# Moving VectorE's sums and output additions to other steps in a fused recurrence and ELU network, with plain products for the last four pairs

## Chip, cores and metric

One Trainium2 chip, one core. The number that counts is the device time of one execution in microseconds; lower is better. All data are fp32. The engines are named as in the profile: PE (TensorE, with PEld its weight loads), DVE (VectorE), ACT (ScalarE), POOL (GpSimd) and SP (SyncE, which only issues DMAs here).

## What is computed

```python
# q, k, v, f_logit: (4, 8, 768, 48)
f = 1.0 / (1.0 + np.exp(-f_logit))
for t in range(S):
    state = f[:, :, t, :, None] * state + np.einsum('bhd,bhe->bhde', k[:, :, t], v[:, :, t])
    y[:, :, t] = np.einsum('bhd,bhde->bhe', q[:, :, t], state)
x = y.transpose(0, 2, 1, 3).reshape(3072, 384)
h = x @ w_in                                   # 384 -> 2048
g = np.where(h > 0.0, h, np.exp(np.minimum(h, 0.0)) - 1.0)
out = g @ w_out                                # 2048 -> 384
```

A gated recurrence gives x for 3072 tokens; two matrix products with an ELU between them follow. "The second product" below is `g @ w_out`.

## The kernel before, in words

**Units, pairs, steps.** The tokens are cut into 12 units of 256 (`m` = 0 to 11). The 2048 hidden features make 16 tiles of 128, taken two at a time, so a unit has 8 pairs (`j` = 0 to 7). A pair over all units has the number P = 8m + j, 0 to 95. The main loop runs over steps T = 0 to 191; step T = 2P makes the first product of pair P (`up`), step 2P + 1 finishes that pair's hidden sums (`joined`) and makes the second product of pair P − 2 (`down`, `LAG = 2`). The place of a step in its unit is called **s = T mod 16** below.

**The order of the work is written by hand.** Each engine executes its instructions in the order in which the program emits them (`manual_schedule`), and waits on semaphores where data or a buffer is missing. `plan` (filled by `at_step`) says which work of the recurrence is emitted at which step. For units 3 to 11 it is, one unit ahead: decays at s = 9, 11, 13, 15 (DVE: a scan and a reciprocal; POOL: scalings of k and q), the x differences `blend` at s = 13 (POOL), `transposed` at s = 2 (PE and ACT), `both` at s = 5 (PE: state updates and scores; DVE: `mask` and `step`), `outputs` at s = 9 and `carried` at s = 11 (PE and ACT). Reading the weights once more for a range check takes ACT at s = 2, 6, 10 and 14 (`check`).

**First product, units 1 to 11.** `up7` multiplies in two groups: 4 products into a PSUM tile `pa`, 6 into `pb`, by a scheme with fewer products than a plain one. ACT copies one result out of `pa` (`u1`), DVE adds it (`hh`, line 965), and after `pb` `joined` makes three more DVE additions (line 978). ACT then applies Relu and Exp to 512 columns (lines 988 and 989), and at the next even step DVE finishes the ELU (`elu`, line 1010) with one `scalar_tensor_tensor` into the tile `gg`. `pa` and `pb` share two PSUM buffers, so `pa` of the next pair waits for the `hh` addition of this one, and `pb` of the next for `joined` of this one.

**Second product, units 2 to 11.** Two pairs at a time are a quad Q. Its second product is done by a bilinear scheme: sums of parts of `gg` (the tile `sums`, names a0 to a13) are multiplied by prepared sums of w_out (b0 to b13) or by parts of w_out, and 16 results c0 to c15 accumulate over the four quads in the four PSUM banks m0 to m3. `PRODUCTS[0]` (10 products) runs at the quad's first `down`, `PRODUCTS[1]` (9 instructions) at its second. The sums of `gg` come from three tables: `SUMS_OF_TWO` (4 rows, POOL, after the ELU of the quad's first pair), `SUMS_SOON` (3 rows, DVE) and `SUMS_OF_FOUR` (8 rows, POOL), both after the ELU of the second pair. Each row is one 128x128 `tensor_tensor` at line 1026 (`combined`). Since `elu(P - 1)` is called inside `up7(P)`, the three DVE rows stand in DVE's queue ahead of `joined(P)`.

**Output of a unit.** After a unit's last `down`, `ended` has ACT copy the four banks to SBUF (`kept`, and `last` for c12 to c15), at s = 4 of the next unit. The 22 rows of `OUTPUTS` are additions on DVE that make the six output blocks o0 to o5 out of c0 to c15; they wait in the list `pending` and are emitted 4 at a time (`SPREAD`) at the odd steps s = 7, 9, 11, 13, 15 and 1, then the store on SP's queue. In unit 11 they are emitted 5 at a time. The last unit is ended at once after the last product, with the rows of `OUTPUTS_AT_THE_END` on DVE and POOL and with its last two `down` calls cut 7 and 12; its store is issued by SP and ACT after the flag of the range check has been read.

Units 0 and 1 (`m < PLAIN`) make the second product plainly: two 128x384 accumulations in two banks.

Of the kernel before, what the change touches and what calls it, by code (L numbers as in the profile page):

```python
# [8 lines left out]
FP32 = mybir.dt.float32  # L9
# [3 lines left out]
AF = mybir.ActivationFunctionType  # L13
ALU = mybir.AluOpType
# [341 lines left out]
def table(text):  # L356
    return [tuple(row.split()) for row in text.split(",") if row.strip()]
# [5 lines left out]
SUMS_OF_TWO = table(  # L363
    "a0 x0 - x1, a1 a0 - x4, a2 x5 + a1, a3 x0 - x4, "
)
SUMS_SOON = table(
    "a7 x4 + x2, a10 x2 - x7, a5 x2 - x6, "
)
SUMS_OF_FOUR = table(
    "a12 a0 + x7, a4 x6 - x7, a6 x5 + a4, a9 x4 + x6, a13 x0 + x2, a8 x1 + x2, a8 a8 - x3, a11 x3 - x7, "  # L370
)
# [5 lines left out]
PRODUCTS = (  # L377
    table(
        "x4 b10 c0 1, x5 w5 c11 1, x1 b12 c14 1, a0 b1 c2 1, a1 b8 c1 1, a2 w3 c7 1, a3 b6 c3 1, x2 b5 c5 1, "
        "x7 b9 c6 1, a7 b3 c4 1, "  # L380
    ),
    table(
        "a10 b4 c8 1, a5 w6 c10 1, a12 b7 c9 1, a4 b13 c11 1, a9 b11 c15 1, a6 b0 c15 1, a13 b2 c13 1, "
        "a8 w10 c13 2, a11 w9 c12 1, "
    ),
)
OUTPUTS = table(
    "o0 c3 + c12, o1 c4 - c13, o2 c3 - c14, c1 c0 + c1, c2 c2 - c1, c5 c4 - c5, c8 c8 + c5, c9 c9 - c2, "
    "c7 c7 - c9, c10 c10 - c8, o0 o0 + c6, o0 o0 + c8, o0 o0 - c9, o1 o1 + c3, o1 o1 + c2, o2 o2 + c5, "
    "o2 o2 - c1, o3 c6 + c7, o3 o3 - c10, o5 c11 - c0, o5 o5 - c10, o4 c7 - c15, "  # L390
)
OUTPUTS_AT_THE_END = table(
    "c1 c0 + c1, c2 c2 - c1, o1 c3 + c2, o2 c3 - c1, c5 c4 - c5, o1 o1 + c4, o2 o2 + c5, c9 c9 - c2, "
    "c8 c8 + c5, c7 c7 - c9, o5 c11 - c0, c10 c10 - c8, o3 c6 + c7, o0 c3 + c8, o5 o5 - c10, "
    "o3 o3 - c10, o0 o0 - c9, o0 o0 + c6, o4 c7 - c15, o1 o1 - c13, o2 o2 - c14, o0 o0 + c12, "
)


# [2 lines left out]
def fast(ctx: ExitStack, tc: tile.TileContext, q, k, v, f_logit, w_in, w_out, out, flag, outer):  # L401
# [18 lines left out]
    nc = tc.nc  # L420
    B, H, D, S = q.shape
    DM = H * D
# [4 lines left out]
    NW = U // W  # L427
    NC = U // C
    UPB = S // U
    NU = B * UPB  # L430
    HP = H // 2
    NFT = DFF // 128
    NKT = DM // 128
    PAD = 64 - D
    NP = NFT // 2
    DH = DM // 2
    NQ = NFT // 4
    DIRECT = 1
    PLAIN = 2
    SPREAD = 4  # L440
    LAG = 2
    AHEAD = 7
    WA = 1
# [438 lines left out]
    def at_step(step, *todo):  # L882
        plan.setdefault(step, []).extend(todo)
# [101 lines left out]
    def exped(P, h):  # L985
        m, j = order[P]
        g = gs[P] = sb.tile([128, 2, U], FP32, tag="gg", name=f"gg{m}_{j}", bufs=4)
        nc.scalar.activation(g[:], h, AF.Relu, scale=-1.0)  # L988
        nc.scalar.activation(g[:], g[:], AF.Exp, scale=-1.0)  # L989
        phs[P] = h  # L990

    def up(P):

# [13 lines left out]
    def elu(P):  # L1007
        m, j = order[P]
        g = gs[P]
        nc.vector.scalar_tensor_tensor(  # L1010
            out=g[:], in0=g[:], scalar=-1.0, in1=phs.pop(P), op0=ALU.add, op1=ALU.max
        )
        if m < PLAIN:
            return
        Q = P // 2
        if P % 2 == 0:
            ss[Q] = sb.tile([128, 14, 128], FP32, tag="sums", name=f"sums{m}_{j // 2}")
        for engine, rows in ((nc.gpsimd, SUMS_OF_TWO),) if P % 2 == 0 else (
            (nc.vector, SUMS_SOON), (nc.gpsimd, SUMS_OF_FOUR)
        ):  # L1020
            for row in rows:
                combined(engine, lambda name: hidden(Q, name), row)

    def combined(engine, at, row):
        to, x, sign, y = row
        engine.tensor_tensor(out=at(to), in0=at(x), in1=at(y), op=ALU.add if sign == "+" else ALU.subtract)  # L1026

    def hidden(Q, name):
        i = int(name[1:])
        if name[0] == "a":  # L1030
            return ss[Q][:, i]
        t, f = divmod(i, 4)
        return gs[2 * Q + f // 2][:, f % 2, t * 128 : (t + 1) * 128]
# [9 lines left out]

    def down(P):
        m, j = order[P]
        if m < PLAIN:
            if j == 0:
                pms[m] = [
                    ps.tile([128, DM], FP32, tag=f"m{i}", name=f"psM{m}_{i}") for i in ((0, 3) if m else (1, 2))
                ]  # L1050
            pm, g = pms[m], gs.pop(P)
            for i in range(2):
                for t in range(NW):
                    nc.tensor.matmul(
                        pm[t][:], lhsT=g[:, i, t * 128 : (t + 1) * 128], rhs=wo[:, 2 * j + i, :],
                        start=(j == 0 and i == 0), stop=(j == NP - 1 and i == 1),
                    )
            if j == NP - 1:
                o = (outer if (NU - m) % 2 else sb).tile([128, 2, DM], FP32, tag="o", name=f"o{m}", bufs=1)
                for t in range(NW):  # L1060
                    nc.scalar.copy(o[:, t], pm[t][:])
                    t0 = m * U + t * 128
                    nc.sync.dma_start(out=out[t0 : t0 + 128, :], in_=o[:, t])
                del pms[m]
            return
        Q = P // 2
        if j == 0:
            pms[m] = [ps.tile([128, 4, 128], FP32, tag=f"m{i}", name=f"psM{m}_{i}") for i in (3, 0, 1, 2)]
            begun.clear()
        pm = pms[m]  # L1070
        todo = PRODUCTS[j % 2]
        if m == NU - 1 and j >= NP - 2:
            todo = PRODUCTS[0][:7] if j < NP - 1 else PRODUCTS[0][7:] + PRODUCTS[1]
        for x, y, c, count in todo:
            bank, at = divmod(int(c[1:]), 4)
            count = int(count)
            nc.tensor.matmul(  # L1077
                pm[bank][:, at : at + count], lhsT=hidden(Q, x), rhs=weight(j // 2, y, count),
                start=bank not in begun, stop=(j == NP - 1), skip_group_check=True,
            )  # L1080
            begun.add(bank)
        if j % 2:
            gs.pop(P - 1), gs.pop(P), ss.pop(Q)
        if j == NP - 1 and m < NU - 1:
            soon.append(lambda: ended(m))
        elif j == NP - 1:
            ended(m)

    begun = set()
    soon, pending = [], []  # L1090

    def ended(m):
        pm = pms.pop(m)
        o = (outer if (NU - m) % 2 else sb).tile([128, 2, DM], FP32, tag="o", name=f"o{m}", bufs=1)
        kept = sb.tile([128, 12, 128], FP32, tag="kept", name=f"kept{m}", bufs=1)
        last = spare[:, NQ * 128 : (NQ + 4) * 128].rearrange("p (c f) -> p c f", c=4) if m < NU - 1 else pm[3]
        for b in range(3 if m == NU - 1 else 4):
            nc.scalar.copy(kept[:, 4 * b : 4 * b + 4] if b < 3 else last, pm[b][:])  # L1098

        def at(name):  # L1100
            i = int(name[1:])
            if name[0] == "o":
                return o[:, i // 3, i % 3 * 128 : (i % 3 + 1) * 128]
            return kept[:, i] if i < 12 else last[:, i - 12]

        def store(*queues):
            for t in range(2):
                for h in ((1, 0) if t else (0, 1)):
                    queues[t].dma_start(
                        out=out[m * U + t * 128 : m * U + (t + 1) * 128, h * DH : (h + 1) * DH],  # L1110
                        in_=o[:, t, h * DH : (h + 1) * DH],
                    )

        if m < NU - 1:
            pending.extend(lambda row=row: combined(nc.vector, at, row) for row in OUTPUTS)
            pending.append(lambda: store(nc.sync, nc.sync))
            return
        for row in OUTPUTS_AT_THE_END:
            combined(nc.gpsimd if row[0] in ("o3", "o5") else nc.vector, at, row)
        left.append(store)  # L1120

    low = cst.tile([128, 1], FP32, name="low")
# [133 lines left out]
    for n in range(NR):  # L1256
        t = 3 * NFT + (NU - 4) * NFT * n // NR + RR
        at_step(t, lambda n=n: reread(n))
        at_step(t + 4, lambda n=n: check(n))
    at_step((NU - 1) * NFT + 9, lambda: finish_flag(0))  # L1260
    at_step((NU - 1) * NFT + 13, lambda: finish_flag(1))
    for T in range(NU * NFT):
        P = T // 2
        sevens = order[P][0] >= DIRECT
        if T % 2 and sevens:
            joined(P)
        if T % 2 == 0 and P and order[P - 1][0] < DIRECT:
            elu(P - 1)
        for f in plan.pop(T, ()):
            f()  # L1270
        if T % 2 == 0:
            up(P)
        elif P >= LAG and T not in joint:
            if T - 2 in joint:
                down(P - LAG - 1)
            down(P - LAG)
        for n in later.pop(T, ()):
            split(n)
            if n not in (A1[2], A1[2] + 1):
                lower(n)  # L1280
        if T % 2 == 0:
            while soon:
                soon.pop()()
        elif T % (2 * NP) not in (3, 5):
            now = SPREAD + (P >= (NU - 1) * NP)
            for f in pending[:now]:
                f()
            del pending[:now]
    elu(NU * NP - 1)
    for P in range(NU * NP - LAG, NU * NP):  # L1290
        down(P)
# [50 lines left out]
```

## Time and profile before

| what | value |
|---|---|
| median of 3 runs | 586.39 us (586.38 to 587.2) |
| the profiled execution's own time | 589.72 us |
| its span | 588.0 us |
| PE busy | 554.5 us (94% of the span) |
| DVE busy | 467.8 us (80%), 1006 instructions |
| POOL busy | 385.9 us (66%), 715 instructions |
| ACT busy | 279.7 us (48%), 601 instructions |
| granted PE clock over the span | 0.992 |

A row of groups reads: line, engine, operation, tiles (out<-in), size, count, then the union of busy time, the mean of one, the idle time of the engine just before these instructions, and who ended it. In a row of the timeline the first number is the start in us, the second the length of the merged stretch. An fp32 product of 128 by 128 by 128 is two MATMUL rows, 0.223 us together in the timeline's spacing. "L1026" is the line of the helper `combined`, so the sums of `gg` and the output additions are told apart by their tiles: `sums<-...` and `o<-...`, `kept<-...`.

### The profile page before, as it was taken

Reading aid. Unit: us, or ns where it says so; the run is one execution under the profiler, and the core shown is the slowest. Engines: PE = TensorE matmul, PEld = TensorE weight load, DVE = VectorE, ACT = ScalarE, POOL = GpSimd, SP = SyncE. Lnnn points to the kernel's source line nnn. Section 1 sums busy time; section 2 is a strip of 40 time slices with the busy share of each in tenths; the row PEclk is TensorE's granted clock in tenths of the full one; section 3 lists DMA queues with packets and bytes.
Section 4 is the critical chain, followed back from the end, with each engine's and each line's share of the span. In section 5 each row is a group of like instructions: output and inputs, shape, how many; then the busy total and the mean of one; then the engine's idle time right before and its main releaser. Section 6 shows DMA issues by size and latency. Waiting matters only on the chain. (4 is left out here: it accounts for less than half of the span.)

```text
span 588.0 us, 16718 instructions
## 1 busy us (share of the span) xinstructions
PE 554.5 (94%) x6698; PEld 499.7 (85%) x6698; DVE 467.8 (80%) x1006; ACT 279.7 (48%) x601; POOL 385.9 (66%) x715
## 2 busy tenths in 40 slices
PE   6789989999999999999999999999999999999993
PEld 3466767779999998988988998998998998899992
DVE  8788975766677896896896896896897797777695
ACT  3287845333535536536445545544553644544431
POOL 6600898477686595686587577678578479447564
PEclk9999989999999999999999999999999999999997
DMA  8999961051053054044136117108108103201001
GB/s 204 241 241 235 251 169 41 3 129 35 2 118 101 6 134 119 17 110 133 29 76 169 29 41 203 30 14 230 30 8 219 45 9 79 73 12 52 1 15 48
DMA packets 39192, 54.37 MB, mean 92 GB/s; under 512 B 4000, under 2 KB 28928, under 8 KB 39104
## 3 DMA queue, kind: packets, MB, share of 16 engines
q1 hardware_dynamic: 38304, 52.61, 35.0%
q8 instruction: 55, 0.90, 0.6%
q10 hardware_dynamic: 800, 0.59, 0.5%
q14 instruction: 33, 0.27, 0.1%
HBM read 45.02 MB, written 4.72 MB: 85 GB/s over the span
## 5 line engine op out<-in xcount | busy, mean ns | idle before, releaser
L956 PE MATMUL psH<-xt,wi 128*128 128x128 f32 (+1 forms) x1056 | 197.2, 296 | 1.9 <-DVE hh L965 0.6
L988 ACT ACTIVATE gg<-hh 128x512 f32<-128x512 f32 x88 | 55.5, 631 | 247.2 <-DVE hh L978 187.7
L956 PEld LDWEIGHTS psH<-xt,wi 128*128 128x128 f32 x1056 | 147.0, 192 | 7.2 <-DVE hh L965 4.3
L956 PE MATMUL psH<-xt,area 128*128 128x128 f32 x704 | 124.3, 279 | 9.4 <-DVE hh L978 7.3
L956 PEld LDWEIGHTS psH<-xt,area 128*128 128x128 f32 x704 | 106.7, 192 | 18.8 <-PE psH L956 10.0
L1077 PE MATMUL psM<-area,sums 128*128 128x128 f32 x720 | 119.9, 278 | 0.6
L1026 POOL TENSOR_TENSOR sums<-gg 128x128 f32<-128x128 f32 x160 | 79.6, 498 | 59.3 <-DVE gg L1010 51.1
L965 DVE TENSOR_TENSOR hh<-psH,u 128x256 f32<-128x256 f32 x88 | 36.8, 418 | 89.0 <-ACT u L963 88.8
L1026 POOL TENSOR_TENSOR sums<-sums,gg 128x128 f32<-128x128 f32 x120 | 58.8, 490 | 72.4 <-DVE gg L1010 66.1
L1077 PEld LDWEIGHTS psM<-area,sums 128*128 128x128 f32 x720 | 98.8, 192 | 2.8 <-POOL sums L1026 2.2
L1077 PE MATMUL psM<-wo,sums 128*128 128x128 f32 (+1 forms) x320 | 64.0, 302 | 0.6 <-POOL sums L1026 0.6
L685 DVE RECIPROCAL f<-f 128x256 f32<-128x256 f32 x36 | 62.8, 1747 | 1.1
L1010 DVE SCALAR_TENSOR_TENSOR gg<-gg,hh 128x512 f32<-128x512 f32 x88 | 62.1, 705 | 1.1 <-POOL sums L1026 1.1
L989 ACT ACTIVATE gg<-gg 128x512 f32<-128x512 f32 x96 | 60.5, 630 | 3.0
L1026 POOL TENSOR_TENSOR sums<-gg,gg 128x128 f32<-128x128 f32 x120 | 58.3, 514 | 0.0
L978 DVE TENSOR_TENSOR hh<-psH,u43h 128x256 f32<-128x256 f32 (+1 forms) x176 | 54.7, 352 | 3.0
L1077 PE MATMUL psM<-area,gg 128*128 128x128 f32 x320 | 56.6, 279 | 0.0
L1077 PEld LDWEIGHTS psM<-wo,sums 128*128 128x128 f32 x320 | 51.5, 191 | 3.2 <-POOL sums L1026 1.0
L675 POOL TENSOR_TENSOR k<-k,f 128x256 f32<-128x256 f32 x48 | 36.1, 755 | 20.6 <-DMA f<-f 7.5
L675 POOL TENSOR_TENSOR q<-q,f 128x256 f32<-128x256 f32 x48 | 36.6, 764 | 18.4 <-DMA area<-in_moe_w_in_dram 15.5
L1077 PEld LDWEIGHTS psM<-area,gg 128*128 128x128 f32 x320 | 45.3, 192 | 0.9 <-ACT spare L1098 0.2
L1026 POOL TENSOR_TENSOR sums<-gg,sums 128x128 f32<-128x128 f32 x80 | 41.4, 517 | 6.3
(113 smaller groups left out, 883.0 us busy)
## 6 DMA issues: line engine op xcount, KB each, us to landing
area<-in_moe_w_out_dram SPq DMA_DIRECT2D x8, 768.0 KB, 11.1
again<-in_moe_w_in_dram SPq DMA_DIRECT2D x16, 384.0 KB, 3.4
again<-in_moe_w_out_dram SPq DMA_DIRECT2D x16, 384.0 KB, 3.8
k<-in_k_dram SPq DMA_DIRECT2D x12, 384.0 KB, 4.9
q<-in_q_dram SPq DMA_DIRECT2D x12, 384.0 KB, 5.6
v<-in_v_dram SPq DMA_DIRECT2D x12, 384.0 KB, 5.9
area<-in_moe_w_in_dram SPq DMA_DIRECT2D x8, 576.0 KB, 10.0
out_dram<-o SPq DMA_DIRECT2D x38, 96.0 KB, 3.5
```

The costliest lines, as they stand in the source:

```text
L675: e.tensor_tensor(out=t[n][:, p], in0=t[n][:, p], in1=t["f"][:, p, "kq".index(n)], op=ALU.mult)
L685: nc.vector.reciprocal(f[:, p, 1], f[:, p, 0])
L956: nc.tensor.matmul(to, lhsT=lhs, rhs=rhs, start=(n == 0), stop=True, skip_group_check=True)
L965: add = lambda to, x, y: nc.vector.tensor_tensor(out=to, in0=x, in1=y, op=ALU.add)
L978: add = lambda to, x, y: nc.vector.tensor_tensor(out=to, in0=x, in1=y, op=ALU.add)
L988: nc.scalar.activation(g[:], h, AF.Relu, scale=-1.0)
L989: nc.scalar.activation(g[:], g[:], AF.Exp, scale=-1.0)
L1010: nc.vector.scalar_tensor_tensor(out=g[:], in0=g[:], scalar=-1.0, in1=phs.pop(P), op0=ALU.add, op1=ALU.max)
L1026: engine.tensor_tensor(out=at(to), in0=at(x), in1=at(y), op=ALU.add if sign == "+" else ALU.subtract)
L1077: nc.tensor.matmul(pm[bank][:, at : at + count], lhsT=hidden(Q, x), rhs=weight(j // 2, y, count), start=bank not in begun, stop=(j == NP - ...
```

## The change

1. **SUMS_SOON.** Of a unit's four quads, the first and the last (s = 4 and s = 0 at their second ELU) keep the three rows on DVE, but they are put in a list `behind` and emitted at the end of the following odd step, after `joined` and whatever `plan` has there. For the two middle quads (s = 8 and s = 12) the three rows go to POOL, ahead of its eight. The product with a7 moves from `PRODUCTS[0]` to `PRODUCTS[1]`, which makes 9 and 10 instructions.
2. **Output additions.** The 23 entries of `pending` are emitted by the table `ROOM`: 3, 5 and 2 at s = 6, 7, 8, and 3, 3, 4 and 3 at s = 0, 1, 2, 3. In unit 11 they are 4 at each step from T = 180 on, and 6 at each from T = 188 on. At an even step they stand behind `elu` and ahead of the next `joined`.
3. **Last four pairs.** In unit 11 only pairs 0 to 3 (two quads) use the bilinear scheme; `ended` follows at T = 188 with the same `OUTPUTS` as every unit. Pairs 4 to 7 are plain, into banks a0 and a1, which the recurrence no longer needs there; after the last product DVE adds each of the two 128x384 banks to the output blocks that are there already. The ELU of the very last pair, with its Relu and Exp, is done in two halves of 256 columns, one per group of 128 tokens, and the plain products run token group by token group.
4. **The flag.** Its two parts are emitted at s = 7 and 10 of unit 11 in place of 9 and 13, as its product uses bank a0.

```diff
@@ PRODUCTS
-        "x7 b9 c6 1, a7 b3 c4 1, "
+        "x7 b9 c6 1, "
...
-        "a10 b4 c8 1, a5 w6 c10 1, ...
+        "a7 b3 c4 1, a10 b4 c8 1, a5 w6 c10 1, ...
@@ constants
-    SPREAD = 4
+    ROOM = {6: 3, 7: 5, 8: 2, 0: 3, 1: 3, 2: 4, 3: 3}
@@ exped
-        nc.scalar.activation(g[:], h, AF.Relu, scale=-1.0)
-        nc.scalar.activation(g[:], g[:], AF.Exp, scale=-1.0)
+        for to, frm in halves(P, g[:], h):
+            nc.scalar.activation(to, frm, AF.Relu, scale=-1.0)
+            nc.scalar.activation(to, to, AF.Exp, scale=-1.0)
+    def halves(P, *tiles):
+        if P < NU * NP - 1:
+            return [tiles]
+        return [[x[:, :, t * 128 : (t + 1) * 128] for x in tiles] for t in range(NW)]
@@ elu
-        for engine, rows in ((nc.gpsimd, SUMS_OF_TWO),) if P % 2 == 0 else (
-            (nc.vector, SUMS_SOON), (nc.gpsimd, SUMS_OF_FOUR)
-        ):
-            for row in rows:
-                combined(engine, lambda name: hidden(Q, name), row)
+        at = lambda name: hidden(Q, name)
+        shared = P % (2 * NQ) in (1, 7)
+        for row in SUMS_OF_TWO if P % 2 == 0 else SUMS_OF_FOUR if shared else SUMS_SOON + SUMS_OF_FOUR:
+            combined(nc.gpsimd, at, row)
+        if P % 2 and shared:
+            behind.extend(lambda row=row: combined(nc.vector, at, row) for row in SUMS_SOON)
+
+    def plain(P):
+        m, j = order[P]
+        return m < PLAIN or m == NU - 1 and j >= NP // 2
@@ down
-        if m < PLAIN:
+        if plain(P):
+            first = NP // 2 if m == NU - 1 else 0
+            if j == first:
+                tags = ("m1", "m2") if m == 0 else ("m0", "m3") if m < NU - 1 else ("a0", "a1")
+                whole[m] = [ps.tile([128, DM], FP32, tag=tag, name=f"psM{m}_{tag}") for tag in tags]
+            pm, g = whole[m], gs.pop(P)
+            for t, i in ((t, i) for t in range(NW) for i in range(2)):
+                nc.tensor.matmul(
+                    pm[t][:], lhsT=g[:, i, t * 128 : (t + 1) * 128], rhs=wo[:, 2 * j + i, :],
+                    start=(j == first and i == 0), stop=(j == NP - 1 and i == 1),
+                )
...
+                    if m == NU - 1:
+                        nc.vector.tensor_tensor(out=o[:, t], in0=pm[t][:], in1=o[:, t], op=ALU.add)
+                        continue
...
-        if j == NP - 1 and m < NU - 1:
+        if j == last:
             soon.append(lambda: ended(m))
-        elif j == NP - 1:
-            ended(m)
@@ ended: all four banks are copied and OUTPUTS goes to pending for unit 11 too
@@ flag
-    at_step((NU - 1) * NFT + 9, lambda: finish_flag(0))
-    at_step((NU - 1) * NFT + 13, lambda: finish_flag(1))
+    at_step((NU - 1) * NFT + 7, lambda: finish_flag(0))
+    at_step((NU - 1) * NFT + 10, lambda: finish_flag(1))
@@ main loop
-        elif T % (2 * NP) not in (3, 5):
-            now = SPREAD + (P >= (NU - 1) * NP)
-            for f in pending[:now]:
-                f()
-            del pending[:now]
+        else:
+            while behind:
+                behind.pop(0)()
+        now = (4 if T < NU * NFT - 4 else 6) if P >= (NU - 1) * NP else ROOM.get(T % (2 * NP), 0)
+        for f in pending[:now]:
+            f()
+        del pending[:now]
```

## The prediction

> **What bounds the kernel now.** First the page's busy times, then busy time in stretches of one unit each, from `pa` at s = 4 to the next `pa` at s = 4.
>
> ```profile
> PE   554.5 (94%) x6698; PEld 499.7 (85%) x6698; DVE 467.8 (80%) x1006; ACT 279.7 (48%) x601; POOL 385.9 (66%) x715
> ```
> ```profile
> 136.70:179.80 43.10, 43.10 (x559) 41.65 (x558) 31.00 (x65) 16.85 (x39) 33.28 (x61) 1.00 0.28 75
> 179.80:224.30 44.50, 43.75 (x577) 41.88 (x575) 37.36 (x85) 21.87 (x54) 31.44 (x61) 1.00 0.31 81
> ...
> 316.40:362.40 46.00, 44.60 (x574) 42.16 (x574) 38.71 (x89) 22.59 (x55) 31.87 (x61) 1.00 0.33 87
> ```
>
> Columns: stretch, length, then busy PE, PEld, DVE, ACT, POOL, the clock, DMA. PE bounds the middle at full clock. The first stretch (unit 2's products) has no output additions yet: 43.10 us, PE never idle. The usual unit takes 46.05, six such in a row 45.9 to 46.2. So about 3 us per unit is PE waiting. The timeline says where. In steps from one `pa` to the next, s = 4→6→...→4:
>
> no additions: 4.56 6.99 5.96 5.94 4.67 4.66 5.56 4.76
> usual unit: 5.42 7.18 5.96 5.94 4.68 5.13 6.53 5.21
>
> The loss sits at s = 14 to 6. DVE's timeline there:
>
> ```profile
> 346.30 0.85 DVE L680 TENSOR_TENSOR_SCAN f<-f 128x256 f32<-128x256 f32 x1
> 347.19 1.75 DVE L685 RECIPROCAL f<-f 128x256 f32<-128x256 f32 x1
> 348.86 1.42 DVE L1026 TENSOR_TENSOR o<-o,kept 128x128 f32<-128x128 f32 x4
> 350.20 0.41 DVE L965 TENSOR_TENSOR hh<-psH,u 128x256 f32<-128x256 f32 x1
> ...
> 355.22 0.43 DVE L1026 TENSOR_TENSOR sums<-gg,gg 128x128 f32<-128x128 f32 x1
> 355.57 1.54 DVE L1026 TENSOR_TENSOR sums<-gg 128x128 f32<-128x128 f32 x2
> 357.04 0.41 DVE L978 TENSOR_TENSOR u43h<-psH,hh 128x256 f32<-128x256 f32 x1
> ```
>
> DVE has no gap from 343.1 to 358.8: reciprocal and four additions together put `hh` at 350.20, and PE pays:
>
> ```profile
> 352.35 0.68 PE L956 MATMUL psH<-xt,area 128*128 128x128 f32 x4 [0.52 <-DVE hh L978]
> ```
>
> The lateness travels on: Relu at s = 2 starts at 358.20, ACT copies `u1` at 361.66, and the `hh` of s = 2 comes at 361.93. POOL is the second in line. Its queue in the same place:
>
> ```profile
> 344.22 0.56 POOL L1026 TENSOR_TENSOR sums<-sums,gg 128x128 f32<-128x128 f32 x1 [1.89 <-DVE gg L1010]
> ...
> 347.90 0.46 POOL L1026 TENSOR_TENSOR sums<-gg 128x128 f32<-128x128 f32 x1
> 348.31 3.21 POOL L944 TENSOR_TENSOR xt<-xt 128x128 f32<-128x128 f32 x5
> ...
> 354.52 0.97 POOL L1026 TENSOR_TENSOR sums<-gg 128x128 f32<-128x128 f32 x1
> ...
> 360.89 0.46 POOL L1026 TENSOR_TENSOR sums<-gg 128x128 f32<-128x128 f32 x1
> ```
>
> It runs without a gap from 344.22 to 361.35. The sum at 354.52 (a3) is wanted by PE at 355.3: even now PE waits 0.24 for it at s = 1, and in the stretch without additions 0.23.
>
> **What the Trainium skill says.** "GPSIMD Engine Reference", Specifications: GpSimd's SBUF interfaces are shared with VectorE, with contention when a DVE instruction has two SBUF inputs. The trace agrees: a POOL sum takes 0.46 alone, 0.84 beside the scan and 0.97 beside `elu`; an output addition repeats every 0.20 alone, and in the five-row stretches of the last unit every 0.36. "VectorE: DVE Perf Modes", The TRN2 errata: the cost of an SBUF instruction has a fixed part, so half the width is not half the time. The trace agrees for two widths: Relu takes 0.63 at 512 columns, ACT copies 0.38 at 256.
>
> **The change, part by part.** Times are counted from `pa` at s = 4.
>
> *DVE's relief (parts 1 and 2).* At s = 9 to 15, 14 additions and the three sums of s = 12 leave DVE. The chain that remains: scores end 4.65 (PE); mask 1.2, states 1.85, the moved sums 0.6 (POOL idle there, three at 0.20) → 8.3; `hh` 0.34, `elu` 0.6, three additions 1.1 (at 0.36), `joined` 1.0 → 11.35; Relu and Exp 1.3, gates 1.65, `u1` 0.3 → 14.6; `hh`, `elu`, two additions 0.7, `joined` → 17.3; Relu and Exp, ACT's small copies 0.25, check 1.25, `u1`, `hh`, `elu`, `joined` → 22.35; Relu and Exp, the xt copies 1.8, `u1`, `hh`, `elu` 0.7 → 26.8. In the usual unit that `elu` (s = 12) ends at 344.22 − 316.36 = 27.86. From there DVE has only `joined`, scan and reciprocal: `joined` of s = 15 ends near 32.2, and `pb` of s = 0 wants it at 33.7. So the waits at s = 14 and 0 go; those two steps become 4.66, and 5.56 before what follows.
>
> *POOL is late next.* Its queue from 26.8: eight sums took 4.09 (344.22 to 348.31), three more at 0.42 give 5.35 → 32.15; `blend` 2.8 (166.75 to 169.50 in the unit without additions, 3.18 beside additions) → 34.95; k and q of s = 13, 1.4 → 36.35; a0 to a3, 2.1 → 38.45. PE starts `pa` of s = 0 at 32.78, and wants a0 at 32.78 + 2.44 + three products at 0.223 = 35.9, a3 0.67 later. It waits for a3 to 38.5, then three products 0.67 and the transposes 0.66: `pa` of s = 2 at 39.85. That step is 7.1 long, 0.57 more than now. Then POOL's settle 2.2 and eight sums 3.75 → 44.4, and PE's ten products at s = 3 end at 39.85 + 2.44 + 2.44 = 44.75: just covered. `hh` at s = 2 follows the transposes: copies 1.15 → 41.0, check, `u1` → 42.5, `hh`, `elu`, four additions 1.44, `joined` → 45.9, against 45.65 wanted by `pb` of s = 4.
>
> The unit becomes 4.8 + 6.99 + 5.96 + 5.94 + 4.67 + 4.66 + 7.1 + 4.9 = **45.0**. So of 3 us lost, 2 come back from DVE and POOL takes one away. Bounds: with POOL's rows at their fastest it is 44.2 (the unit without additions plus about 1.1); if POOL's and DVE's rows all run at their contended price, 46.4.
>
> The a7 product, moved behind its sum, costs nothing: PE does as many products, and a7 is ready at 8.0 where it is wanted at 9.2 (s = 7, behind the first nine). The three POOL sums of s = 8 are covered too: 15.6 + 5.35 = 21.0, their last product at 23. The store, from s = 1 to s = 3, lies on SP ahead of the reread of s = 6 and of later loads, and nothing near waits for these. The banks' copies at s = 4 now wait for the rows of s = 3; `scores` wants two of them at 3.5 and has them by about 3.4, which may cost some tenths.
>
> *Sum over units.* Six usual units: 276.2 − 6 × 45.0 = −6.2. The stretch 179.8 to 224.3 (44.5) gains no DVE wait at s = 0: +0.5. The unit without additions gets the three sums on POOL: +1.0. The last stretch (43.2, no decays) loses only its wait of 0.76 at s = 5, of which I take 0.5: −0.5. Together **−5.2**.
>
> *The end (parts 3 and 4).* From T = 180 four additions stand ahead of each `joined`, and the first four wait for the last bank's copy (3.4 after `pa`). With the flag's 0.9, the chain `joined` to `joined` at T = 184 is 5.7, PE's pair 4.66: +1.4 until T = 188 (0.2 if rows run at 0.2, 2.2 at 0.4). From `pa` of T = 188 (563.41 now) the end is: PE 2.44, four plain products of 0.646 (323 ns a row, twice), up 2.44, three times 2.58, in all 15.3 if DVE keeps up (`joined` at 5.7 to 6 against 5.93 wanted, last ELU half at 12.6 to 13 against 13.95). Then one 384-wide addition, about 0.55 (0.42 at 256 columns, 0.68 at 512, both from PSUM): 16.05. Now ACT's stores go out 581.28 − 563.41 = 17.87 after it, so −1.8. There the plain form costs 1.4 more PE time (16 × 0.646 against 8.9), but the bank copies and the additions behind the last product go. The last DMA lands 5.4 after its data now; two of four stores leave earlier, −0.4 (0 to −1). Together **−0.8** (−2.8 to +1.2).
>
> *Total:* −6.0: span 588.0 → 582.0, the profiled execution 589.7 → 583.7. That execution stands 3.3 above the median; taken off the median, **580.4 us**.
>
> **Rivals.**
> 1. *POOL takes it all back, slower.* The price is contention: in s = 0 to 3 DVE gets 12 additions and 3 sums beside POOL's 15 rows, where now it has 3 or 4 additions. For it: 0.77 for a scaling and 0.54 to 0.58 for a sum beside DVE, and the 0.23 wait with none. If each POOL row there is 0.12 longer than taken, 1.3 to 1.8 per unit appear at the one place where PE already waits (a3, s = 1): unit 46.35, +1.35 on seven units, −6.0 + 9.4 = +3.4: **589.8**. It decides from about 0.85 per unit on. Against it: DVE also leaves POOL alone at s = 9 to 15.
> 2. *POOL keeps up.* If `elu` at s = 12 comes a microsecond earlier (additions at 0.2 in the chain to 26.8), unit 44.2: −6.0 − 7 × 0.8 = **574.8**.
> 3. *A draw*, 586: POOL loses 0.85 per unit.
>
> **How the numbers follow.** My forecast 0.58 (own range 577 to 584), rival 2 0.12, rival 1 0.18, the draw 0.12. A difference under 0.2% (1.2 us) can't be told from none. Range 574.8 to 588.5: it holds rival 2's value and the draw, and leaves out most of rival 1. Faster 0.71, within 0.2% 0.11, slower 0.18.
>
> **What would show it.** Right: no PE wait on L978 at s = 0; `psM` weight loads waiting for POOL's sums at s = 1, about 1 to 2 us per unit; units of 44.6 to 45.4; POOL without a gap from s = 12 to s = 3. Wrong: units at 46 or more with that wait over 2.5 us, or a wait for DVE at s = 4 of over 0.5; at the end, PE waits on L978 at T = 184 to 190 above 2.5 us in all.

## The result and the profile after

| | before | after |
|---|---|---|
| median | 586.42 us (585.23 to 588.19, 12 runs) | 586.13 us (584.59 to 589.29, 12 runs) |
| ratio after / before | | 0.9993, 95% interval 0.9976 to 1.0011 |
| profiled execution, its span | 589.72 us, 588.0 us | 585.22 us, 583.5 us |

No measurable change. The forecast was 580.4 us. The two profiled executions differ by 4.5 us, and that is no evidence of a gain: a second profiled execution of each kernel gave 585.22 us for before and 588.14 us for after, the other way round.

The page's row of busy times for the kernel after:

```profile
PE 558.4 (96%) x6654; PEld 496.9 (85%) x6654; DVE 446.6 (77%) x950; ACT 280.9 (48%) x604; POOL 398.8 (68%) x744
```

DVE is down by 21 us of busy time and POOL up by 13. Yet PE, which bounds the middle, is busy 4 us longer with 44 rows fewer. Part of it is the wider plain products of the last unit; and a PE stretch of four rows that takes 0.61 us elsewhere is shown as 1.02 where sums come late (below), so busy PE is no measure of PE's speed here.

Busy time by stretch after, in the columns of the prediction's table (stretch, length, PE, PEld, DVE, ACT, POOL, clock, DMA); the rows are unit 2's stretch without additions, the next, and a usual unit:

```profile
133.90:178.20 44.30, 44.07 (x560) 41.97 (x558) 29.32 (x59) 17.52 (x39) 35.57 (x67) 1.00 0.27 73
178.20:223.30 45.10, 44.39 (x577) 41.99 (x576) 34.95 (x76) 21.66 (x54) 34.59 (x68) 1.00 0.28 74
314.10:359.90 45.80, 44.70 (x576) 42.12 (x576) 37.09 (x83) 22.70 (x55) 34.69 (x68) 1.00 0.34 88
```

The stretch without additions got longer, 43.10 to 44.30; the next, 44.50 to 45.10. POOL has 2.3 us more in the first of them. The usual unit gained only tenths: six in a row have a mean of 45.56 after and 46.03 before. The prediction had 45.0.

The places where PE loses time after the change lie in the steps s = 0 and s = 4. PE's timeline of one usual unit, whose `pa` of s = 0 starts at 347.77 and `pa` of s = 4 at 359.94:

```profile
347.77 0.39 PE L951 MATMUL psH<-xt,wi 128*128 128x128 f32 x2
348.55 0.49 PE L951 MATMUL psH<-xt,area 128*128 128x128 f32 x2 [0.39 <-POOL xt L939]
...
351.31 0.39 PE L1085 MATMUL psM<-area,gg 128*128 128x128 f32 x2
351.72 1.02 PE L1085 MATMUL psM<-area,sums 128*128 128x128 f32 x4
...
360.39 0.61 PE L951 MATMUL psH<-xt,wi 128*128 128x128 f32 x4
361.51 0.68 PE L951 MATMUL psH<-xt,area 128*128 128x128 f32 x4 [0.51 <-DVE hh L973]
```

Three waits are to be seen: at 348.55 for `xt`, the output of POOL's `blend`; from 351.5 on for POOL's sums a0 to a3, where four MATMUL rows that take 0.61 elsewhere stretch over 1.02; and at 361.51 for `joined` of s = 3. The waits at s = 14 and s = 0 behind DVE's reciprocal are gone. DVE's timeline of the same steps shows what is ahead of `joined` now:

```profile
349.82 0.42 DVE L960 TENSOR_TENSOR hh<-psH,u 128x256 f32<-128x256 f32 x1 [2.38 <-ACT u L958]
350.16 1.20 DVE L1012 SCALAR_TENSOR_TENSOR gg<-gg,hh 128x512 f32<-128x512 f32 x1
351.28 1.60 DVE L1031 TENSOR_TENSOR o<-o,kept 128x128 f32<-128x128 f32 x3
352.81 0.41 DVE L973 TENSOR_TENSOR u43h<-psH,hh 128x256 f32<-128x256 f32 x1
...
357.70 0.42 DVE L960 TENSOR_TENSOR hh<-psH,u 128x256 f32<-128x256 f32 x1 [1.03 <-ACT u L958]
358.05 0.74 DVE L1012 SCALAR_TENSOR_TENSOR gg<-gg,hh 128x512 f32<-128x512 f32 x1
358.71 0.54 DVE L1031 TENSOR_TENSOR o<-o,kept 128x128 f32<-128x128 f32 x1
359.17 0.54 DVE L1031 TENSOR_TENSOR o<-kept 128x128 f32<-128x128 f32 x1
```

The `elu` of s = 0 takes 1.20 us where it takes 0.68 alone, and three additions take 1.6 where they repeat every 0.20 alone. POOL's timeline shows the other side of the same collision, and that POOL has not paused since s = 12:

```profile
341.46 0.46 POOL L1031 TENSOR_TENSOR sums<-gg,gg 128x128 f32<-128x128 f32 x1 [1.33 <-DVE gg L1012]
...
346.97 2.47 POOL L939 TENSOR_TENSOR xt<-xt 128x128 f32<-128x128 f32 x5
349.40 0.72 POOL L670 TENSOR_TENSOR k<-k,f 128x256 f32<-128x256 f32 x1
350.08 0.73 POOL L670 TENSOR_TENSOR q<-q,f 128x256 f32<-128x256 f32 x1
350.76 0.91 POOL L1031 TENSOR_TENSOR sums<-gg 128x128 f32<-128x128 f32 x1
```

`blend` ends at 349.40, which is 1.6 us after PE began the step whose products read `xt`. The q scaling, begun 0.08 us ahead of the long `elu`, keeps its own time of 0.73; the sum a0 behind it, begun while `elu` runs, takes 0.91 where 0.46 is its time alone.

### The profile page after: what moved, and what is told of

Same layout as the page of the kernel before. It is cut to its first block, busy times and chain, and to the rows that moved or that the text cites. A ratio compares the mean times of both kernels' runs of the same rounds, so it can differ in the third digit from the quotient of the medians.

```text
span 583.5 us, 16622 instructions
## 1 busy us (share of the span) xinstructions
PE 558.4 (96%) x6654; PEld 496.9 (85%) x6654; DVE 446.6 (77%) x950; ACT 280.9 (48%) x604; POOL 398.8 (68%) x744
## 4 chain that ended last, share of the span: by engine, by line
PE 33%; DVE 26%; ACT 18%; POOL 11%; issue 6%; DMA 3%; SPq 0%; ACTq 0%; POOLq 0%; DVEq 0%
PE psH L951 14%; POOL sums L1031 8%; PE psM L1085 6%; DVE o L1031 6%; PE psM_m L1058 4%; DVE gg L1012 4%; DVE hh L973 4%; ACT gg L984 3%; POOL xt L939 3%; DVE hh L960 3%; DVE u43h L973 2%; ACT area L624 2%; PE psU_a L781 2%; PE psM_a L1058 2%; PE psS L758 2%
## 5 line engine op out<-in xcount | busy, mean ns | idle before, releaser
L984 ACT ACTIVATE gg<-hh 128x512 f32<-128x512 f32 (+1 forms) x89 | 55.7, 626 | 239.1 <-DVE hh L973 188.7
L1031 POOL TENSOR_TENSOR sums<-gg 128x128 f32<-128x128 f32 x190 | 98.4, 524 | 26.7 <-DVE gg L1012 26.7
L1085 PE MATMUL psM<-area,sums 128*128 128x128 f32 x684 | 112.1, 280 | 0.6
L1085 PEld LDWEIGHTS psM<-area,sums 128*128 128x128 f32 x684 | 92.1, 192 | 5.5 <-POOL sums L1031 4.9
L1031 POOL TENSOR_TENSOR sums<-sums,gg 128x128 f32<-128x128 f32 x114 | 64.1, 562 | 26.8 <-DVE gg L1012 20.9
L1012 DVE SCALAR_TENSOR_TENSOR gg<-gg,hh 128x512 f32<-128x512 f32 (+1 forms) x89 | 69.6, 783 | 0.3 <-ACT gg L985 0.3
L985 ACT ACTIVATE gg<-gg 128x512 f32<-128x512 f32 (+1 forms) x97 | 60.7, 626 | 3.1
L1085 PEld LDWEIGHTS psM<-wo,sums 128*128 128x128 f32 x304 | 48.3, 191 | 6.8 <-POOL sums L1031 5.1
L670 POOL TENSOR_TENSOR k<-k,f 128x256 f32<-128x256 f32 x48 | 40.1, 838 | 16.2 <-DVE f L675 5.8
L1058 PE MATMUL psM_m<-wo,gg 128*128 128x384 f32 x128 | 44.2, 489 | 0.0
```

Source lines behind the costliest of these rows:

```text
L670: e.tensor_tensor(out=t[n][:, p], in0=t[n][:, p], in1=t["f"][:, p, "kq".index(n)], op=ALU.mult)
L984: nc.scalar.activation(to, frm, AF.Relu, scale=-1.0)
L985: nc.scalar.activation(to, to, AF.Exp, scale=-1.0)
L1012: nc.vector.scalar_tensor_tensor(out=to, in0=to, scalar=-1.0, in1=h, op0=ALU.add, op1=ALU.max)
L1058: nc.tensor.matmul(pm[t][:], lhsT=g[:, i, t * 128 : (t + 1) * 128], rhs=wo[:, 2 * j + i, :], start=(j == first and i == 0), stop=(j == NP ...
L1085: nc.tensor.matmul(pm[bank][:, at : at + count], lhsT=hidden(Q, x), rhs=weight(j // 2, y, count), start=bank not in begun, stop=(j == last ...
```

## Experiments

**The theories.** Theory A: two limits of about the same size stand in the same place after the change. One is POOL's queue, which the three more sums at s = 12 push into s = 0 and 1. The other is DVE's queue at s = 0 to 3, where output additions now stand ahead of `joined`. Each hides the other, so taking away one gives a part, and both give more than the sum. The rivals put the loss on one of the two alone, or on the end of the program.

All runs in one table. "Unit" is the mean of six usual units (T = 68 to 164), "s = 0→2" and "s = 4→6" are steps of one usual unit, "no add." is the stretch T = 36 to 52, and the last two columns are the time from `pa` of T = 180 to `pa` of T = 188 and from there to the end of the span; times in us. A ratio stands against the kernel before in the same runs. The change moves one product of each quad (a7) to the next odd step, here from s = 1 to s = 3; in before, before_again, rows_alone and rows7_alone it is still at s = 1, so their s=0→2 holds about 0.22 us more work than that of the others.

| kernel | time | ratio, 95% interval | unit | s=0→2 | s=4→6 | no add. | T=180→188 | to end |
|---|---|---|---|---|---|---|---|---|
| before | 586.42 | 1 | 46.03 | 6.53 | 5.42 | 43.10 | 19.85 | 24.47 |
| before_again | 585.22, one run | | 46.05 | 6.53 | 5.42 | 43.10 | 19.84 | 22.88 |
| after | 586.13 | 0.9993 (0.9976 to 1.0011) | 45.56 | 6.62 | 5.32 | 44.31 | 22.38 | 21.43 |
| after_again | 588.14, one run | | 45.60 | 6.62 | 5.32 | 44.33 | 22.38 | 22.47 |
| sums_alone | 584.02 | 0.9969 (0.9954 to 0.9984) | 45.38 | 7.58 | 4.57 | 44.33 | 19.25 | 22.68 |
| rows_alone | 606.58 | 1.0386 (1.0328 to 1.0444) | 48.57 | 6.08 | 6.48 | 43.10 | 21.30 | 22.53 |
| end_alone | 587.68 | 1.0035 (1.0016 to 1.0054) | 46.03 | 6.31 | 5.43 | 43.10 | 22.66 | 22.07 |
| few_rows | 573.21, one run | | 44.46 | 6.73 | 4.60 | 44.32 | 19.87 | 20.16 |
| sums12_dve | 580.55, one run | | 44.87 | 5.21 | 5.85 | 43.19 | 22.01 | 21.96 |
| rows_at7 | 582.95, one run | | 44.89 | 6.72 | 4.57 | 44.51 | 21.30 | 22.88 |
| both_moves | 570.54 | 0.974 (0.9713 to 0.9767) | 43.64 | 5.15 | 4.59 | 43.19 | 21.25 | 22.04 |
| rows7_alone | 583.42, one run | | 45.56 | 6.10 | 5.24 | 43.09 | 20.24 | 22.71 |
| after_end8 | 584.87, one run | | 45.58 | 6.62 | 5.32 | 44.52 | 21.11 | 22.04 |
| moves_old_end | 568.01 | 0.9699 (0.9671 to 0.9728) | 43.64 | 5.16 | 4.57 | 43.18 | 19.25 | 23.21 |

The mean unit is a far steadier measure than the total: it repeats within 0.04 us between two executions of one kernel, in the two kernels that were profiled twice. The stretch up to T = 36, in which the kernels differ at most in the order of the plain products of units 0 and 1, lies between 132.7 and 136.7 us from execution to execution. So the single totals say little by themselves, and the readings below go by units.

**The same two kernels once more.** No edit.

> The kernel before once more, unchanged, for its trace: units of 45.9 to 46.2 and 44.3 from T = 180 to the last instruction as in the first trace, within 0.1. The stretch up to T = 36 was 136.7 there and 132.8 to 135.6 in eight other traces, where no other kernel differs from before up to there in anything but the order of the plain products: if it is 133 to 135 now, the first trace of before was long by about 2 us in the start.

> The kernel after once more, unchanged: units of 45.4 to 45.9 and 43.8 from T = 180 on, and 133 to 136 up to T = 36. If the start of before and after has the same spread, the change's effect is that of T = 36 to the end: 449.6 against 451.3, which is 0.3% or 1.7 us less.

The units came out as the first time (46.05 and 45.60); the end, forecast to repeat within 0.1 us for before, did not. What differed was the start (136.7 and 133.6 us to T = 36 for before, 133.9 and 135.5 for after) and the stretch from T = 188 to the end (24.47 and 22.88 for before, 21.43 and 22.47 for after). From T = 36 to 180, before takes 406.95 and 407.07, after 405.78 and 406.10: on the mean the loop gained 1.07 us, where −5.2 had been forecast.

**Each part by itself.** *sums_alone* is the kernel before with part 1 of the change in units 2 to 10, and also in unit 11 except for the very last pair's ELU:

```diff
-        for engine, rows in ((nc.gpsimd, SUMS_OF_TWO),) if P % 2 == 0 else (
-            (nc.vector, SUMS_SOON), (nc.gpsimd, SUMS_OF_FOUR)
...
+        shared = P % (2 * NQ) in (1, 7) and P < NU * NP - 1
...
+        if P % 2 and shared:
+            behind.extend(lambda row=row: combined(nc.vector, at, row) for row in SUMS_SOON)
```

> The kernel before with the new places of the three sums (and of the a7 product) and nothing else; the last quad's sums stay as they were. Theory A: the four rows behind each reciprocal stay, but DVE is rid of the three sums at s = 12 and of those ahead of joined at s = 0: usual unit 45.2 to 45.8. Rival B (the three sums on POOL at s = 12 are what costs): 46.0 or more, with over 1.5 us per unit of psM weight loads waiting for POOL's sums at s = 1.

It is faster than before by 0.31% and its unit, 45.38, is shorter than that of the whole change. The wait at s = 4 is gone (4.57), while s = 0→2 went up to 7.58, the highest of all kernels. PE's timeline of *sums_alone* at s = 0:

```profile
302.59 0.39 PE L956 MATMUL psH<-xt,wi 128*128 128x128 f32 x2
303.74 0.49 PE L956 MATMUL psH<-xt,area 128*128 128x128 f32 x2 [0.77 <-POOL xt L944]
...
307.09 1.02 PE L1081 MATMUL psM<-area,sums 128*128 128x128 f32 x4 [0.19 <-POOL sums L1030]
308.28 0.49 PE L1081 MATMUL psM<-wo,sums 128*128 128x128 f32 x2 [0.17 <-POOL sums L1030]
```

With the three sums no longer ahead of `joined`, the waits left in this step are POOL's: first for its `blend`, then for its sums.

*rows_alone* is the kernel before with part 2 alone up to T = 180:

```diff
+    ROOM = {6: 3, 7: 5, 8: 2, 0: 3, 1: 3, 2: 4, 3: 3}
...
-        elif T % (2 * NP) not in (3, 5):
-            now = SPREAD + (P >= (NU - 1) * NP)
+        if T >= (NU - 1) * NFT + 4:
+            now = (SPREAD + 1) * (T % 2 == 1 and T % (2 * NP) not in (3, 5))
+        else:
+            now = ROOM.get(T % (2 * NP), 0)
```

> The kernel before with the new places of the output additions (ROOM) and nothing else; the three sums stay on DVE ahead of joined, the end is as before. Theory A (the change took the wait behind the reciprocals away, and it came back as DVE rows ahead of joined at s = 0 and 2, and as POOL's longer queue): the waits at s = 14 go, POOL has only eight sums at s = 12, but three rows and three sums stand ahead of joined at s = 0: usual unit 45.3 to 45.8 us where before has 46.05 and the change 45.43. Rival B (POOL's three more sums at s = 12 alone took the gain back): without them the unit is 44.3 or less.

It is 20 us slower than before, and its unit of 48.57 misses the forecast of 45.3 to 45.8 by far. Its PE waits, and DVE's timeline at s = 0 (columns of a wait: who waits, for whom, us in total, times, longest):

```profile
PE psH L957 <- DVE hh L979: 24.7, 23, 1.6
```
```profile
213.04 0.43 DVE L1027 TENSOR_TENSOR sums<-gg,gg 128x128 f32<-128x128 f32 x1
213.39 1.27 DVE L1027 TENSOR_TENSOR sums<-gg 128x128 f32<-128x128 f32 x2
214.59 2.01 DVE L1027 TENSOR_TENSOR o<-o,kept 128x128 f32<-128x128 f32 x3
216.52 0.41 DVE L979 TENSOR_TENSOR u43h<-psH,hh 128x256 f32<-128x256 f32 x1
```

Three sums and three additions between `elu` and `joined` take 3.5 us, and PE pays for it 23 times. So the additions at even steps are tolerable only because part 1 takes the sums away from there. The forecast had named these six rows and still expected a gain.

*end_alone* is the kernel after with part 2 undone for the units before the last and the sums of part 1 put back ahead of `joined` everywhere (only the a7 product stays moved). The part of its edit that restores the additions:

```diff
-        now = (4 if T < NU * NFT - 4 else 6) if P >= (NU - 1) * NP else ROOM.get(T % (2 * NP), 0)
+        now = (4 if T < NU * NFT - 4 else 6) if P >= (NU - 1) * NP else SPREAD * (T % 2 == 1 and T % (2 * NP) not in (3, 5))
```

> The kernel after with the sums and the additions of units 2 to 10 put back as they were before: only the plain last pairs, their additions from banks a0 and a1, the halved last ELU, unit 11's rows and the earlier flag remain. From the two profiles: usual units 46.05 as before; T = 180 to 188 about 22.4 where before has 19.85 and 188 to the end about 21.4 where before has 24.5, so -0.5 in all. If the 0.93 that PE waits at T = 180 in the changed kernel comes from unit 10's rows ahead of joined at s = 0 and 2 it falls outside this stretch here as well, and T = 180 to 188 is 21.5.

It is slower than before by 0.35%. The end as written costs more at T = 180 to 188 (22.66 against 19.85) than it brings behind; the forecast had it bring 0.5 us in all. It is not quite the end of the change: at T = 186 PE waits 1.45 us for `joined` here and 0.22 in the change, since in *end_alone* three sums stand ahead of an odd step's `joined` together with four additions.

**One of the two limits taken out of the change.** *few_rows* keeps 6 of the 22 additions and leaves the others out, so its output lacks their terms; it serves for the times alone:

```diff
-    "o0 c3 + c12, o1 c4 - c13, o2 c3 - c14, c1 c0 + c1, c2 c2 - c1, c5 c4 - c5, c8 c8 + c5, c9 c9 - c2, "
-    "c7 c7 - c9, c10 c10 - c8, o0 o0 + c6, o0 o0 + c8, o0 o0 - c9, o1 o1 + c3, o1 o1 + c2, o2 o2 + c5, "
-    "o2 o2 - c1, o3 c6 + c7, o3 o3 - c10, o5 c11 - c0, o5 o5 - c10, o4 c7 - c15, "
+    "o0 c3 + c12, o1 c4 - c13, o2 c3 - c14, o3 c6 + c7, o5 c11 - c0, o4 c7 - c15, "
...
-    ROOM = {6: 3, 7: 5, 8: 2, 0: 3, 1: 3, 2: 4, 3: 3}
+    ROOM = {6: 3, 7: 4}
```

> The kernel after with 16 of the 22 output additions of each unit left out (the six that write each output block first remain, three at s = 6 and three at s = 7), so the output is not the reference's. Theory A: no rows are left at s = 0 to 3, so no wait for joined at s = 4 (0.74 now) and less contention for POOL; POOL's queue from s = 12 remains: usual unit 44.2 to 44.6 where the change has 45.43. Rival B (POOL's queue alone is the limit): 45.0 or more. If the unit falls to 43.3, the limit was the rows alone.

The unit falls by 1.1 us to 44.46, all of it where additions stood ahead of `joined` or beside POOL (s = 4→6 from 5.32 to 4.60, s = 2→4 from 5.27 to 4.91), and s = 0→2 stays at 6.73. The weight loads of the second product still wait for POOL:

```profile
PEld psM L1083 <- POOL sums L1029: 7.8, 32, 0.4
```

The additions therefore account for 1.1 us of the unit's loss against 43.10, and POOL for most of the rest, since the loss that stays is at s = 0→2.

*sums12_dve* gives the three sums of s = 12 back to DVE, behind `joined`:

```diff
-        shared = P % (2 * NQ) in (1, 7)
+        shared = P % (2 * NQ) in (1, 5, 7)
```

> The kernel after with the three sums of s = 12 on DVE as well, behind joined and the reciprocal of s = 13, so that POOL has eight there and not eleven. Theory A (POOL's queue and DVE's rows ahead of joined are two limits of the same size at s = 0 to 4: taking one away lets PE run into the other): the steps from s = 0 to 2 fall from 6.62 to about 5.7, the wait at s = 4 grows from 0.74 to about 1.5, usual unit 44.8 to 45.3 us (45.43 in the change). Rival B (POOL's queue alone holds PE): the unit falls by the whole 1.26, to 44.2.

*rows_at7* leaves the sums and puts all additions behind `joined`:

```diff
-    ROOM = {6: 3, 7: 5, 8: 2, 0: 3, 1: 3, 2: 4, 3: 3}
+    ROOM = {6: 3, 7: 10, 8: 2, 1: 4, 3: 4}
```

> The kernel after with its additions in other places: 3 at s = 6, 10 at s = 7, 2 at s = 8, 4 at s = 1 and 4 at s = 3, none ahead of joined at s = 0 and 2. Theory A: no PE wait for joined at s = 4, POOL's queue stays the limit as with few rows: usual unit 44.4 to 44.8. Rival B: 45.2 to 45.4, since POOL has the same work; what would speak for DVE time as such (not the place) is a unit of 45.4.

Both bring the same: 44.87 and 44.89, that is 0.7 us per unit. The first lies in the range of Theory A, the second 0.1 above it. They bring it in different steps. The PE waits of *sums12_dve*, and the weight loads' waits of *rows_at7*:

```profile
PE psH L951 <- DVE hh L973: 7.9, 9, 1.0
```
```profile
PEld psM L1085 <- POOL sums L1031: 9.7, 39, 0.4
...
PEld psH L951 <- POOL xt L939: 3.3, 8, 0.7
```

With the sums back on DVE, s = 0→2 falls to 5.21, 1.4 us shorter, but PE then reaches s = 4 earlier and waits longer for the same `joined`: s = 4→6 rises to 5.85. With the additions moved, that wait goes (4.57) and POOL's remain (6.72).

*both_moves* makes both edits:

> Both of these together: POOL has eight sums at s = 12, and no additions stand ahead of joined at s = 0 and 2. Theory A: both limits are gone: usual unit 43.4 to 44.0 us, against 43.10 for the unit without additions; over eight units 10 to 15 us less than before, 571 to 576. If it stays at 44.4 or more, a third limit is there that I haven't named.

The unit is 43.64, 1.92 us below the change, where the two single effects add up to 1.4. It is close to the 43.10 us of the stretch that has no additions. The whole kernel takes 0.974 of the time of before. Its busy times in a usual unit, then its DVE timeline at s = 0:

```profile
264.40:308.00 43.60, 43.38 (x561) 41.78 (x559) 37.18 (x85) 23.09 (x57) 33.66 (x65) 1.00 0.34 92
```
```profile
299.20 0.68 DVE L1012 SCALAR_TENSOR_TENSOR gg<-gg,hh 128x512 f32<-128x512 f32 x1
300.12 0.42 DVE L973 TENSOR_TENSOR u43h<-psH,hh 128x256 f32<-128x256 f32 x1 [0.23 <-PE psH L951]
```

`joined` now waits for PE, not PE for `joined`; DVE does as much work in the unit as in the change (37.18 and 37.09). And the two waits of PE in question are nearly gone:

```profile
PE psH L951 <- DVE hh L973: 0.2, 1, 0.2
```
```profile
PEld psM L1085 <- POOL sums L1031: 3.1, 8, 0.4
```

**The moved rows on the kernel before.** *rows7_alone* is the kernel before with the `ROOM` of *rows_at7* and nothing else:

> The kernel before with only the additions in the places of rows_at7 (3, 10, 2, 4, 4 at s = 6, 7, 8, 1, 3); the three sums stay on DVE ahead of joined. Theory A (what counts is DVE time ahead of joined, where the places of the sums and of the rows add up): at s = 0 three sums and no rows, at s = 2 nothing, at s = 4 three sums and, behind joined of s = 3, four rows: far better than rows_alone (48.6) and a little better than before: 44.5 to 45.5. Rival (the additions cannot gain anything as long as the sums stay): 46 or more.

The unit is 45.56, 0.47 below before and the same as that of the whole change. The additions behind `joined` bring this without any move of sums: the wait for `joined` at s = 0, behind a reciprocal and four additions in before, is gone, s=0→2 falls from 6.53 to 6.10 and s = 2→4 from 5.21 to 4.66. A wait of 0.50 has come at s = 14 (5.40 in this unit, 5.26 before) and one of 0.44 stays at s = 4, each behind three sums that stand ahead of `joined`.

**The end.** *after_end8* is the change with the additions of unit 10 in unit 11 at 8 per odd step from T = 181 to 187, behind `joined`, in place of 4 at each step, and with those of unit 9 by the table at T = 176 to 179. (In the kernel after, "4 at each step" holds from T = 176 on, when unit 11's first pair begins, and not only from T = 180: four of unit 9's additions stand ahead of `joined` at T = 176 and four at T = 178.)

```diff
-        now = (4 if T < NU * NFT - 4 else 6) if P >= (NU - 1) * NP else ROOM.get(T % (2 * NP), 0)
+        now = (6 if T >= NU * NFT - 4 else (0, 8)[T % 2] * (T > (NU - 1) * NFT + 4) if T >= (NU - 1) * NFT + 4 else ROOM.get(T % (2 * NP), 0)) if P >= (NU - 1) * NP else ROOM.get(T % (2 * NP), 0)
```

> The kernel after with unit 10's additions in unit 11 emitted 8 at a time at the odd steps from T = 181 on (behind joined), and those of unit 9 by the table as in every unit; the middle of the run is the change's. Theory A (at the end too it is rows ahead of joined that PE waits for: 0.93 at T = 180, 0.24, 0.12 and 0.39 at T = 182 to 186 in the changed kernel): T = 180 to 188 falls from 22.4 to about 20.5, the end to the last instruction stays 21.4. Rival (the plain products' place or the bank copies cost it): 22 or more.

T = 180 to 188 falls from 22.38 to 21.11: half of what the change loses there comes back; the forecast was 20.5. Of the rest, 0.7 lies at T = 180 (6.58 against 5.85 before), where PE still waits 0.46 for `joined` behind unit 9's additions; *both_moves*, which has none of them ahead of `joined` at T = 178, has no such wait. What is left after that, about half a microsecond, no run separates.

*moves_old_end* is the kernel before with both moves and its old end:

> The kernel before with the three sums behind joined on DVE at s = 0, 4 and 12 and on POOL at s = 8 alone, the additions 3, 10, 2, 4 and 4 at s = 6, 7, 8, 1 and 3, and the end as before: the bilinear scheme to the last pair, additions at odd steps 5 at a time. Theory A: the middle is that of both_moves (units of 43.5 to 43.8). The end from T = 180 is that of sums_alone, 41.9, and not 43.3 as in both_moves, since the plain last pairs cost more PE time than their shorter tail saves: 1 to 1.5 us less than both_moves, about 569.2. Rival: the plain end is the better one once the rows wait nowhere: 571.5 or more.

It is the fastest version, 568.01 us, 0.9699 of before (0.9671 to 0.9728), and it beats both kernels by 3%. Its unit is that of *both_moves*, 43.64. The middle came out as forecast. Against *both_moves* the end from T = 180 takes 42.46 (41.9 forecast) against 43.29 us, but the two ratios overlap, so which end is better is not settled by these runs. By the last DVE instruction the plain end is 0.5 us earlier (37.28 against 37.78 from T = 180), by the landing of the last store 0.8 later.

## Why the prediction was wrong

- **The cause of the old loss: right.** The waits at s = 14 and s = 0 were DVE's reciprocal, additions and sums, and they are gone. The chain of DVE up to s = 12 came out about as computed (`elu` of s = 12 ends at 27.2 in the unit shown, 26.8 predicted); the steps 6→8 to 14→0 sum to 28.23 against 28.22 predicted. A slip without effect: 16 additions leave s = 9 to 15, four at each odd step, and not 14.
- **POOL is late next: right in kind, and its own step over-charged.** POOL has no pause from s = 12, and 0→2 measures 6.62 in one unit and 6.91 in the unit shown, against 7.1 predicted. But one wait in it had no name: the prediction let PE run until a0 was wanted, and had not set `blend`'s end (its own sum gave 34.95, 2.2 after `pa`) against the products of s = 0 that read `xt`. It ends 1.6 us after `pa` began. Of the 1.76 us by which this step exceeds the 5.15 of *both_moves*, about 0.65 stand ahead of the first sum, and 1.1 in the sums.
- **`joined` at s = 3: the step that failed.** The prediction had it 0.25 us late, with s = 4→6 at 4.8; that step is 5.32 to 5.38. The wait shown is 0.51, in all about 0.7. The prediction's chain for s = 2 starts at the transposes; `joined` of s = 1 is not in it, and at the prediction's prices (0.6 for `elu`, 1.1 for three additions) it would, with Relu and Exp behind it, have been done before the transposes. At s = 0 the two run at 1.12 + 1.53 from start to start, 0.95 longer, and the four additions at s = 2 at 1.59, against 1.44. Together with the 0.39 that PE waited for `xt` this makes `joined` of s = 1 end 6.1 us after `pa` of s = 0 in place of some 4.8 (6.1 − 0.95 − 0.39). ACT's Relu and Exp follow it, so the copies of the transposes end 1.5 us after `pa` of s = 2 where 1.15 had been taken, and `u1` and `hh` behind them are as late. The prediction took an addition beside POOL at 0.36 and `elu` at its price alone, both from steps where POOL had less to do; in the very steps to which the change moves the rows they cost 0.5 and 1.12. *rows_at7* and *both_moves*, where the additions stand behind `joined`, have no such wait. In *rows_at7* `elu` of s = 0 still takes 1.20, so the long `elu` without additions behind it makes no wait.
- **s = 2→4: mis-sized.** 4.9 predicted, 5.27 measured. POOL's sums of s = 3 are not "just covered": they are some tenths late, with DVE's additions beside them. *few_rows*, without those, has 4.91.
- **Sum over units.** Six usual units: −6.2 predicted, −2.8 measured. The stretch without additions +1.22 (+1.0 predicted), the next +0.62 (+0.5), the last −0.13 (−0.5). The total over T = 36 to 180 is −1.07 (−5.2). The small terms were about right, the large one was not. By step, the unit is longer than predicted by 0.53 at s = 4→6 and 0.37 at s = 2→4, and shorter by 0.37 at s = 0→2: the over-charged POOL step hid, by luck, a part of the miss.
- **The end, T = 180 to 188: mis-sized.** +1.4 predicted, +2.53 measured. The wait at T = 180 is not in the sum: unit 9's additions at T = 176 and 178 stand ahead of `joined` there too, four at each, as PE's timeline of after shows at T = 180:

```profile
541.50 0.68 PE L951 MATMUL psH<-xt,area 128*128 128x128 f32 x4 [0.77 <-DVE hh L973]
```

  There the step is 6.88 against 5.85 before, and the bank copies end 5.2 us after `pa`, where the prediction had 3.4. Smaller waits for `joined` follow at T = 182 to 186; over the four steps `pb` starts 1.8 us later in all than it does without a wait.
- **The end, T = 188 on: the work was right, the landing was not.** The plain products and the two wide additions went as computed: the last DVE instruction ends 16.03 us after `pa` of T = 188, where 16.05 was predicted. The agreement to 0.02 is luck, since the prediction's terms (15.3 and 0.55) add up to 15.85. Its pair of widths for the fixed part of a row's cost was a Relu and a copy out of PSUM, two kinds of row; the halves of the last ELU show it for one kind: Relu takes 0.42 at 256 columns and 0.63 at 512, `elu` 0.42 and 0.68. DVE's last two rows and ACT's two stores of after:

```profile
576.24 0.56 DVE L1068 TENSOR_TENSOR o<-psM_a,o 128x384 f32<-128x384 f32 x1 [1.41 <-PE psM_a L1058]
577.52 0.56 DVE L1068 TENSOR_TENSOR o<-psM_a,o 128x384 f32<-128x384 f32 x1 [0.73 <-PE psM_a L1058]
```
```profile
578.11 1.81 ACTq L1115 DMA_DIRECT2D out_dram<-o  x2
```

  The last store landed 5.37 us after its data in the first execution of before, and the prediction took this as the price. A second execution of the same kernel had 3.78; after had 4.08 and 5.11. The spread of one landing is as large as the whole gain forecast there. The 3.3 us by which the profiled execution stood above the median lay partly in it and partly in the start (136.7 us to T = 36, 133.6 in the second execution).
- **Summed up.** From T = 36 to 180 −1.07, and from 180 to the last DVE instruction +0.2; with the mean landings, +0.8 to the end. That gives −0.9 to −0.3 us, and −0.3 was measured with about ±1. The draw of the prediction's third rival occurred, but not by its mechanism of POOL taking 0.85 us back alone. Two collisions share it. DVE's at s = 4 stood only among the signs that would show the forecast wrong (a wait for DVE there of over 0.5), not among the rivals; rival 1 named contention, and put its price on POOL's rows only.

## What to carry to other kernels

When rows move to other steps, give each its price beside the engine that runs there, and do so for both engines: here `elu` went from 0.68 to 1.20 us and a POOL sum from 0.46 to 0.91. Ask too which of the two rows begins first, since here the later one paid (next section). Then walk the chain of every product that reads something of the loaded engine, including inputs such as `blend`'s that had slack before. Two limits of the same size in one place hide each other: each edit alone brought 0.7 us per unit and both brought 1.92, so an edit that "brings little" should be tried together with the next limit before it is dropped; and work that no one waits for belongs behind the instruction that someone does.

## What the runs showed that was not expected

- Where `elu` on DVE and a POOL row meet in these traces, the one that begins later pays. The q scaling of s = 13 began 0.08 us ahead of `elu` in the change: it took 0.73 and `elu` 1.20. In *sums_alone* at T = 96 it began 0.03 us behind `elu`: it took 1.24 and `elu` 0.68. The 128x128 sums do the same on a smaller scale: in *few_rows* at s = 2 a sum that began 0.09 us ahead kept its 0.46, and `elu` took 0.91; in before at s = 0 a sum that began 0.02 us behind took 0.97, and `elu` 0.68. The fourteen traces have 209 `elu` rows between T = 52 and 176 that begin with more than 0.13 us of a POOL row still to run. Of these, 202 take what is left of that row and 0.54 to 0.56 more; in the other seven the two rows begin within 0.01 us of each other, and the POOL row is the longer one. So the 1.20 of the change comes from the order in which the two began and the length of the row ahead. The Trainium skill, "GPSIMD Engine Reference", Specifications, has contention where a DVE instruction has two SBUF inputs, as `elu` has; the runs agree, and show that the price can fall on DVE too, by 0.5 us on one row.
- The landing of the last 96 KB store took from 3.8 to 5.4 us after its data in two executions of the same kernel. ACT's first store of the last pair landed 3.8 to 4.9 us after issue in after, against 3.0 in before; why the first of two stores on that queue lands later in the new form was not tried and stays open.
- The part up to T = 36, the same in all kernels but for the order of the plain products, took 132.7 to 136.7 us in single executions. For a 1 us question one profile's total is too coarse, while the mean of six inner units repeats within 0.04.
